# Two background streams with buffers of their own for the weight gradients and the x gradient in a fused decode-block backward kernel

## The chip, the cores and the metric

The kernel runs on one core of a Trainium2 chip. The metric is the device time of one execution in microseconds. The core has five engines with a queue each, worked through in order: TensorE (PE) multiplies matrices and writes PSUM, VectorE (DVE) and ScalarE (ACT) work elementwise and read PSUM, GpSimd (POOL) and SyncE (SP) mostly issue DMA transfers here. Sixteen DMA engines move data between HBM and the on-chip SBUF.

## What is computed

The reference is a transformer block for one new token per sequence, and its gradients. There are B = 2 sequences, D = 640, 32 heads of 128, a cache of 4096 positions, and a hidden width of 1728.

```
h   = x + attention(layernorm(x) @ wq, k_cache, v_cache) @ wo
out = h + relu(layernorm(h) @ w1) @ w2
grads of out, by grad_out, for x, k_cache, v_cache, wq, wo, w1, w2
```

Outputs are out_0 (out), out_1 (gradient of x), out_2 and out_3 (of the two caches, 64 blocks of 1 MB each), out_4 (wq), out_5 (wo), out_6 (w1) and out_7 (w2), all bf16. The weight gradients are sums of two outer products, one for each sequence.

## The kernel before

**Passes.** A head of a sequence is a pair, and there are 64. The first pass (p1_iter) loads K and V of a pair, makes scores, softmax and the attention output. Two sequences' worth of middle work (middle_gen: output projection, layer norm, the hidden layer and its gradient, and from that the gradient at each head's output, go_group) runs as a background generator. The second pass (p2_iter, L740) loads V of a pair once more as tile W, except for 11 pairs whose V was kept. It transposes W in four groups on PE (t_ps, copied by ACT to t_sb), multiplies each with the head's gradient (dp_ps), and DVE forms the blocks gV and gK as outer products in two halves each (L735). POOL issues their stores (L792, L773). The pass has an iteration j for each pair; the store of gK for pair j stands in iteration j+1. Iterations j = 0 to 10 are interleaved with the first pass, j = 11 to 64 stand alone.

**Background work.** All order is set while the program is written out. p2_iter is a generator with yields between its parts; after each part the loop writes out V loads as far as buffers allow (pump, L998) and then steps of background queues. A queue has a credit that grows by a rate per step; a background generator yields the price of what it wrote out (a plain yield is 0.5), and is called until the credit is used up (bg_step, L945). The counter step[0] counts steps of the second queue, and wait(n) lets n of them pass (2n in the lone second pass). What bg2 holds is fin_gen (L847), at the rate RATE2 = 0.85, from the iteration in which the middle work of the second sequence no longer needs w1.

**What fin_gen does.** rows_of (L799) turns column vectors into rows: ACT widens four columns (L805), PE transposes them (L810), ACT copies them out (L812). outer_rows (L818) makes a weight gradient in groups of rows: a buffer ot of 1 MB or less is taken, PE forms pieces of up to 512 columns (L835), three of them in three PSUM banks, ACT copies the three into ot (L840), and POOL issues the store (L842). The order is out_7, out_6, out_5, the rest of gx, out_1, out_4. Between stores of out_6 and out_5, gx_piece (L856) runs once the heads it needs are done: it loads six heads of wq (tile wqs, L862, from SP), waits 12 steps, transposes 128x128 blocks on PE (L873), ACT copies them (L875), PE multiplies with the query gradient (L885), and DVE adds (L889).

**Buffers.** SBUF has 12 large buffers of 1 MB. They have homes: "ld" for loads (K, V, W, wq, w2 and also ot and wqs) and "g" for gV and gK. take and give move them; a buffer that is given back can be taken at once, and then its next writer waits on the chip until its last reader, or its store, is done. share(4) and share(5) move homes from "ld" to "g" at the start of the lone second pass and at j = 37. `spare` is the number of free "ld" buffers that background work must find (2, from j = 34 on 1), and `reserve` keeps 2 from the V loads from j = 36 on. w1 lies in a pool of its own, wts; when it is released, the pool fin (rows and small tiles) takes its place.

Of the kernel before, what the change touches and what calls it, by code (L numbers as in the profile page):

```python
# [15 lines left out]
def kernel(  # L16
# [60 lines left out]
    homes = {"ld": list(range(NBIG)), "g": []}  # L77
    free = {"ld": NBIG, "g": 0}
    owned = {"ld": NBIG, "g": 0}
    stores = [0]  # L80
    spare = [2]
    home_of = {}

    def take(tag, shape, name):
        assert free[tag] > 0, (tag, name)
        free[tag] -= 1
        k = homes[tag].pop(0)
        t = big.tile(shape, BF16, tag=f"big{k}", bufs=1, name=name)
        home_of[id(t)] = (tag, k, t)
        return t  # L90

    def give(t, to=None):
        tag, k, _ = home_of.pop(id(t))
        to = to or tag
        owned[tag] -= 1
        owned[to] += 1
        free[to] += 1
        homes[to].append(k)

    def share(n):  # L100

        stores[0] = n
        while owned["g"] < n and free["ld"] > 0:
            homes["g"].append(homes["ld"].pop(0))
            for d in (free, owned):
                d["ld"] -= 1
                d["g"] += 1
# [464 lines left out]
    def store_row(col_bf, n, dst):  # L572

        t = pst([16, 128], BF16, "mid", "row_ps")
        nc.tensor.transpose(t[0:n, :], col_bf, ident_bf[:])
        r = small.tile([16, 128], BF16, tag="orow", bufs=1, name="orow")
        nc.vector.tensor_copy(out=r[0:n, :], in_=t[0:n, :])
        nc.sync.dma_start(out=dst, in_=r[0:n, :])
# [47 lines left out]
    def mlp_out():  # L626

        ml32 = small.tile([128, ND, B], FP32, tag="ml32", bufs=1, name="ml32")
        nc.vector.memset(ml32[:], 0.0)
        for k in range(NW2):  # L630
            while free["ld"] < spare[0]:
                yield
            t = load_w2(k, "ld")
            yield from wait(8)
            c1 = min(NF, (k + 1) * FP)
            m_ps = pst([128, ND, B], FP32, "mid", "mlp_ps")
            for c in range(ND):
                for cf in range(k * FP, c1):
                    kc = f_kc(cf)
                    nc.tensor.matmul(m_ps[:, c, :], lhsT=t[0:kc, cf - k * FP, c * 128:(c + 1) * 128],  # L640
                                     rhs=acol[0:kc, cf, :], start=(cf == k * FP), stop=(cf == c1 - 1))
            give(t)
            yield
            nc.vector.tensor_tensor(out=ml32[:], in0=m_ps[:], in1=ml32[:], op=ALU.add)
        ml_bf = small.tile([128, ND, B], BF16, tag="ml_bf", bufs=1, name="ml_bf")
        nc.vector.tensor_copy(out=ml_bf[:], in_=ml32[:])
        y_bf = small.tile([128, B, ND], BF16, tag="y_bf", bufs=1, name="y_bf")
        nc.vector.tensor_tensor(out=y_bf[:].rearrange("p b c -> p c b"), in0=h1c[:], in1=ml_bf[:], op=ALU.add)
        yield from wait(3)
        for b in range(B):  # L650
            store_row(y_bf[:, b, :], ND, out_0[b].rearrange("s (c p) -> (s c) p", p=128))
            yield
# [87 lines left out]
    def p2_iter(j, busy):  # L740
# [45 lines left out]
        give(c["W"], "g" if owned["g"] < stores[0] else "ld")  # L786
# [31 lines left out]
    def outer_rows(L, nrow, R, N, out_ap, cc, between=None):  # L818


        P = nrow // cc
        grp = max(1, min(cc, 4096 // N))
        out_v = out_ap.rearrange("(p c) n -> p c n", c=cc)
        for c0 in range(0, cc, grp):
            gn = min(grp, cc - c0)
            while free["ld"] < spare[0]:
                yield
            ot = take("ld", [128, grp, N], "ot")
            todo = [(k, n0, min(512, N - n0)) for k in range(gn) for n0 in range(0, N, 512)]
            for t0 in range(0, len(todo), 3):  # L830
                part = []
                for k, n0, nn in todo[t0:t0 + 3]:
                    q = 32 * (fw[0] % 4)
                    o_ps = pst([128, 512], FP32, ("mid", "m", "a")[len(part)], "o_ps")
                    nc.tensor.matmul(o_ps[0:P, 0:nn], lhsT=L[q:q + B, bass.ds(c0 + k, P, step=cc)],  # L835
                                     rhs=R[q:q + B, n0:n0 + nn], start=True, stop=True)
                    part.append((o_ps, k, n0, nn))
                    fw[0] += 1
                for o_ps, k, n0, nn in part:
                    nc.scalar.copy(out=ot[0:P, k, n0:n0 + nn], in_=o_ps[0:P, 0:nn])  # L840
                yield 0.5 * len(part)
            nc.gpsimd.dma_start(out=out_v[:, c0:c0 + gn, :], in_=ot[0:P, 0:gn, :])  # L842
            give(ot)
            if between is not None:
                yield from between()

    def fin_gen(fin):  # L847
        gx1 = fin.tile([128, ND, B], FP32, tag="gx1", name="gx1")
        nc.vector.memset(gx1[:], 0.0)
# [3 lines left out]
        yield from wait(4)  # L853
        gx_next = [0]

        def gx_piece(k):  # L856

            hn = min(QP, H - k * QP)
            while free["ld"] < spare[0]:
                yield  # L860
            t = take("ld", [128, ND, QP * 128], "wqs")
            nc.sync.dma_start(out=t[:, :, 0:hn * 128], in_=wq_r[:, :, k * QP * 128:(k * QP + hn) * 128])  # L862
            yield from wait(6)
# [3 lines left out]
            for t0 in range(0, len(todo) + GT, GT):  # L867
                part = todo[t0:t0 + GT]
                nxt = None
                if part:  # L870
                    t_ps = pst([128, GT, 128], BF16, "tps", "t_ps")
                    for x, (c, j) in enumerate(part):
                        nc.tensor.transpose(t_ps[:, x, :], t[:, c, j * 128:(j + 1) * 128], ident_bf[:])  # L873
                    t_sb = mats.tile([128, GT, 128], BF16, tag="XT", bufs=5, name="t_sb")
                    nc.scalar.copy(out=t_sb[:, 0:len(part), :], in_=t_ps[:, 0:len(part), :])  # L875
                    nxt = (t_sb, part)
                    if t0 + GT >= len(todo):
                        give(t)
                    yield 0.9
                if prev is not None:  # L880
                    if acc is None:
                        acc = pst([128, ND, B], FP32, "m", "gx_ps")
# [4 lines left out]
                    yield  # L887
                prev = nxt
            nc.vector.tensor_tensor(out=gx1[:], in0=gx1[:], in1=acc[:], op=ALU.add)  # L889

        def gx_ready():

            k = gx_next[0]
            if k < NQ and all(("go", B - 1, h) in done for h in range(k * QP, min(H, (k + 1) * QP))):
                gx_next[0] += 1
                yield from gx_piece(k)

        yield from rows_of(fin, acol, NF, "ar", "rF")
        yield from rows_of(fin, gc, ND, "gr", "rD")
        yield from outer_rows(FIN["ar"], Dff, FIN["gr"], D, out_7, Dff // 96)  # L900
        yield from rows_of(fin, ghfc, NF, "ghfr", "rF")
        yield from rows_of(fin, x2c, ND, "x2r", "rD")
        yield from outer_rows(FIN["x2r"], D, FIN["ghfr"], Dff, out_6, ND, gx_ready)
        while ("gh1", B - 1) not in done:
            yield
        yield from rows_of(fin, OFc, H, "OFr", "rH")
        yield from rows_of(fin, gh1c, ND, "gh1r", "rD")
        yield from outer_rows(FIN["OFr"], HD, FIN["gh1r"], D, out_5, HD // 128, gx_ready)
        while gx_next[0] < NQ:
            yield from gx_ready()  # L910
# [5 lines left out]
        for b in range(B):  # L916
            gxo = small.tile([128, ND], BF16, tag="gxo", bufs=2, name="gxo")
            nc.vector.tensor_copy(out=gxo[:], in_=gx_bf[:, :, b])
            store_row(gxo[:], ND, out_1[b].rearrange("s (c p) -> (s c) p", p=128))
            yield  # L920
        yield from rows_of(fin, GQc, H, "GQr", "rH")
        yield from rows_of(fin, x1c, ND, "x1r", "rD")
        yield from outer_rows(FIN["x1r"], D, FIN["GQr"], HD, out_4, ND)
# [3 lines left out]
    bg2 = []  # L927
    done = set()
    credit = [0.0, 0.0]
# [15 lines left out]
    def bg_step(k, rate):  # L945
        step[0] += k
        q = (bg, bg2)[k]
# [17 lines left out]
    RATE2 = 0.85  # L965
# [30 lines left out]
    reserve = [0]  # L996

    def pump():  # L998
        while queue:
# [3 lines left out]
            else:  # L1003
                tag = "ld"
                if free["ld"] <= reserve[0]:
# [12 lines left out]
    fin = None  # L1018
# [12 lines left out]
    for n, (i, j) in enumerate(plan):  # L1031
# [3 lines left out]
        if j == 0:  # L1035
            stores[0] = 3
        if i is None and plan[n - 1][0] is not None:
            share(4)
        if j == H + KEPT[1]:
            share(5)  # L1040
# [6 lines left out]
        reserve[0] = 2 if bg2 and j is not None and j >= H + 4 else 0  # L1047
        spare[0] = 1 if j is not None and j >= H + 2 else 2
        if i is None and ("w1", 1) in done and fin is None:
            wts.release()  # L1050
            fin = tc.alloc_tile_pool(name="fin", bufs=1)
            bg2.append(("fin", fin_gen(fin)))
        if i == 12:
# [3 lines left out]
        if i is None:  # L1057
            spread[0] = 2
            k = 0
            while g2 is not None:  # L1060
# [5 lines left out]
                bg_step(1, RATE2)  # L1066
            continue
        at = MIXED if j is not None else REST
        for k, _ in enumerate(p1_iter(i, i < H + 1, int(H + 1 < i < P2_AT))):
# [15 lines left out]
            bg_step(1, RATE2)  # L1085
# [4 lines left out]
    while bg2:  # L1090
        bg_one(bg2)
# [32 lines left out]
```

## Time and profile before

| | |
|---|---|
| median of 13 runs | 1008.92 us (1003.01 to 1024.74) |
| time of the profiled execution | 1012.83 us |
| its span, first to last instruction | 1011.0 us |
| busy: PE, DVE, ACT, POOL | 799.5, 657.3, 586.8, 108.6 us |
| granted TensorE clock, mean | 0.783 |
| moved by DMA | 363.25 MB, 359 GB/s over the span |
| last gV store issued, last gK store issued | 951.43, 959.23 us |
| last weight-gradient store issued | 1004.55 us |
| first weight-gradient copy (out_7) | 701.4 us |
| wqs loads: issue to landing, min/median/max | 17.7/24.6/31.5 us |
| ot stores: issue to landing, min/median/max | 4.1/6.2/19.5 us |

Two views are read together. One gives, for a stretch of the span, each engine's busy time with the number of its instructions, the granted clock, the mean busy share of the DMA engines and the rate at which they moved data. The other, the timeline, gives each instruction's start and length, and in brackets how long its engine was idle before it and what ended that. A line of the waits names an engine and line, what it waited for, the total, the number of times and the longest. Line numbers are those of the code above.

### The profile page before, as it was taken

The page shows a single profiled execution, that of the slowest core. Times are in us where ns is not written, and L with a number is a line of the kernel's source. Part 1 is how long each engine was busy: PE and PEld are TensorE (multiplying, and loading weights), DVE is VectorE, ACT ScalarE, POOL GpSimd, SP SyncE. Part 2 cuts the span into 40 slices and gives each one's busy share as a digit, 9 for nine tenths or more (in the row PEclk, how much of TensorE's full clock was granted, in tenths as well). Part 3 has the DMA queues.
Part 4 walks back from the last instruction along what each step waited for, and adds up shares of the span by engine and source line. Part 5 has one row for each costly group of instructions (what it writes and reads, how often), then busy time and mean ns, then how long its engine had stood idle before and what let it go on. Part 6 is the DMA issues. An engine that isn't in the chain of part 4 may idle for free.

```text
span 1011.0 us, 30245 instructions
## 1 busy us (share of the span) xinstructions
PE 799.5 (79%) x13169; PEld 707.8 (70%) x13173; DVE 657.3 (65%) x1289; ACT 586.8 (58%) x1261; POOL 108.6 (11%) x219
## 2 busy tenths in 40 slices
PE   6999989999899989999886736467487578865846
PEld 5998989988888888888876636356366467654611
DVE  3555766755387668787888798998675456653600
ACT  4566655666667757777754524345365347644747
POOL 0000000000000000000012121112122112210201
PEclk9999997999699979999995856776556557555555
DMA  9999999994677779999999999999799998999735
GB/s 350 419 398 381 361 377 376 364 389 169 218 262 269 287 287 369 422 420 421 405 381 421 424 379 405 426 423 420 307 375 410 420 414 328 421 424 414 300 128 207
DMA packets 63206, 363.25 MB, mean 359 GB/s; under 512 B 5697, under 2 KB 20929, under 8 KB 22881
## 3 DMA queue, kind: packets, MB, share of 16 engines
q1 hardware_dynamic: 42416, 212.18, 54.0%
q0 software_dynamic: 20656, 149.14, 35.6%
q8 instruction: 103, 1.69, 0.6%
q14 instruction: 31, 0.25, 0.1%
HBM read 212.16 MB, written 149.13 MB: 357 GB/s over the span
## 4 chain that ended last, share of the span: by engine, by line
PE 44%; DMA 28%; issue 10%; DVE 10%; ACT 7%; POOL 1%; SPq 0%; POOLq 0%; DVEq 0%; ACTq 0%
PE t_ps L353 11%; PE m_ps L408 11%; DMA wqs<-in_A_wq_dram 10%; DMA out_dram<-gV 8%; DMA out_dram<-gK 7%; PE t_ps L374 5%; PE m_ps L423 5%; ACT t_sb L358 4%; PE s_ps L364 4%; DVE gV L735 4%; DVE gK L735 3%; DMA Kt<-in_A_k_cache_dram 2%; PE dp_ps L387 1%; PE t_ps L345 1%; PE t_ps L873 1%
## 5 line engine op out<-in xcount | busy, mean ns | idle before, releaser
L358 ACT COPY t_sb<-t_ps 128x1024 bf16<-128x1024 bf16 x223 | 219.6, 1014 | 52.7 <-PE t_ps L353 50.4
L379 ACT COPY t_sb<-t_ps 128x512 f32<-128x512 f32 x256 | 148.7, 588 | 114.2 <-PE t_ps L374 111.2
L408 PE MATMUL m_ps<-pk,Vt 128*128 128x129 bf16 x2048 | 204.3, 228 | 4.0 <-issue 4.0
L374 PE MATMUL t_ps<-ident_f,Wt 128*128 128x128 f32 x848 | 186.4, 368 | 2.0 <-DMA Wt<-in_A_v_cache_dram 1.0
L415 DVE TENSOR_TENSOR pk<-Kt,ep 128x2048 bf16<-128x2048 bf16 x128 | 156.0, 1219 | 26.5 <-ACT ep L465 26.5
L735 DVE TENSOR_TENSOR gK<-rb,gsp 128x2048 bf16<-128x2048 bf16 x128 | 152.1, 1227 | 32.1 <-DMA out_dram<-gV 16.9
L735 DVE TENSOR_TENSOR gV<-rb,pp 128x2048 bf16<-128x2048 bf16 x128 | 152.2, 1217 | 22.7 <-DMA out_dram<-gK 11.8
L353 PE MATMUL t_ps<-ident_bf,Kt 128*128 128x128 bf16 x2048 | 158.6, 230 | 4.0 <-issue 2.0
L408 PEld LDWEIGHTS <-Vt 128*128 128x128 bf16 x2048 | 135.6, 103 | 14.3 <-issue 9.0
L374 PEld LDWEIGHTS t_ps<-ident_f,Wt 128*128 128x128 f32 x848 | 132.5, 190 | 16.8 <-issue 8.6
L353 PEld LDWEIGHTS <-Kt 128*128 128x128 bf16 x2048 | 132.3, 103 | 7.2 <-issue 2.9
L387 PEld LDWEIGHTS <-t_sb 128*128 128x128 bf16 x2048 | 92.0, 105 | 50.3 <-ACT t_sb L379 39.7
L387 PE MATMUL dp_ps<-gom,t_sb 128*128 128x2 bf16 x2048 | 94.5, 167 | 23.0 <-ACT t_sb L379 21.9
L364 PE MATMUL s_ps<-qc,t_sb 128*128 128x1 bf16 x2048 | 89.7, 164 | 12.6 <-ACT t_sb L358 8.6
L364 PEld LDWEIGHTS <-t_sb 128*128 128x128 bf16 x2048 | 80.9, 98 | 17.8 <-ACT t_sb L358 12.8
L840 ACT CAST ot<-o_ps 128x512 bf16<-128x512 f32 (+4 forms) x160 | 66.0, 491 | 22.9 <-DMA out_dram<-ot 13.5
L792 POOL DMA_DIRECT2D out_dram<-gV x64 | 34.2, 534 | 386.3 <-DVE gV L735 289.8
L356 DVE COPY t_sb<-t_ps 128x1024 bf16<-128x1024 bf16 x33 | 22.8, 691 | 67.9 <-PE t_ps L353 67.9
L518 ACT ACTIVATE MT<-m_ps,rtot 128x128 bf16<-128x128 f32 x64 | 23.6, 368 | 71.6 <-PE m_ps L408 67.3
L423 PE MATMUL m_ps<-ep,Kt 128*128 128x1 bf16 x2048 | 61.2, 163 | 1.8 <-ACT OU L519 1.2
L773 POOL DMA_DIRECT2D out_dram<-gK x64 | 34.0, 532 | 262.9 <-DVE gK L735 216.9
L423 PEld LDWEIGHTS <-Kt 128*128 128x128 bf16 x2048 | 58.9, 96 | 2.2 <-issue 1.7
(186 smaller groups left out, 878.8 us busy)
## 6 DMA issues: line engine op xcount, KB each, us to landing
Kt<-in_A_k_cache_dram SPq DMA_DIRECT2D x64, 1024.0 KB, 9.7
Vt<-in_A_v_cache_dram SPq DMA_DIRECT2D x64, 1024.0 KB, 8.3
out_dram<-gV POOLq DMA_DIRECT2D x64, 1024.0 KB, 10.9
out_dram<-gK POOLq DMA_DIRECT2D x64, 1024.0 KB, 10.2
Wt<-in_A_v_cache_dram SPq DMA_DIRECT2D x53, 1024.0 KB, 10.7
wo_t<-in_A_wo_dram SPq DMA_DIRECT2D x4, 1280.0 KB, 11.2
out_dram<-ot POOLq DMA_DIRECT2D x5, 1024.0 KB, 4.1
wq_t<-in_A_wq_dram SPq DMA_DIRECT2D x5, 960.0 KB, 9.5
```

Of the source, the lines that this page charges most:

```text
L353: nc.tensor.transpose(t_ps[:, j, :], nat[:, g * GT + j, :], ident_bf[:])
L358: nc.scalar.copy(out=t_sb[:], in_=t_ps[:])
L364: nc.tensor.matmul(dst[:, sc:sc + 1], lhsT=t_sb[:, j, :], rhs=vec, start=True, stop=True)
L374: nc.tensor.transpose(t_ps[:, j, :], natf[:, 2 * cc:2 * cc + 2, :].rearrange("p c k -> p (c k)"), ident_f[:])
L379: nc.scalar.copy(out=t_sb[:], in_=t_ps[:])
L387: nc.tensor.matmul(dst[:, sc:sc + 2], lhsT=v[:, j, :, par], rhs=vecs[:, par, :], start=(par == 0), stop=(par == 1))
L408: nc.tensor.matmul(r["m"][:, 0:129], lhsT=r["V"][:, sc, :], rhs=r["pk"][sc // HALF][:, sc % HALF, 0:129], start=False, stop=(sc == NSC - 1))
L415: nc.vector.tensor_tensor(out=p["pk"][k][:, :, 0:128].rearrange("p s (a two) -> p s a two", two=2), in0=p["K"][:, sl, :].rearrange("p s (a ...
L423: nc.tensor.matmul(r["m"][:, 129:130], lhsT=r["K"][:, sc, :], rhs=r["ep"][:, sc, 0:1], start=(sc == 0), stop=False)
L735: nc.vector.tensor_tensor(out=pairs_view(dst[:, sl, :]), in0=row.rearrange("p (a two) -> p a two", two=2)[:, None, :, :].to_broadcast([128 ...
L792: nc.gpsimd.dma_start(out=natural(out_3, b, h), in_=gV[:])
L840: nc.scalar.copy(out=ot[0:P, k, n0:n0 + nn], in_=o_ps[0:P, 0:nn])
```

## The change

The homes become four: "ld", "g", "f" for weight-gradient buffers (ot) and "q" for wqs and for the w2 tiles of mlp_out. share takes a wanted number for each home, and free or returned buffers move towards it. One more large buffer is added in the pool big2, in w1's old place (fin shrinks, since rows of 4096 columns are made in halves). It is the only "f" buffer until j = 36, when the kept V tiles are used up and the numbers become ld 4, g 4, f 3, q 2; when both streams have ended they become ld 7, g 6. A buffer of "f" is taken only 13 steps after it was given back.

fin_gen loses gx, which becomes gx_gen on a third queue, bg3, with the rate 0.45; RATE2 is 0.65. gx_gen starts when all heads are done and takes a "q" buffer and loads the next piece of wq whenever one is free. outer_rows makes one piece at a time in the bank "m"; gx's sums use the bank "a". From when all heads are done (late), DVE makes every third copy. Stores of ot are issued by ACT instead of POOL. out_5 and out_4 are made in two halves of 16 heads, and out_4 no longer stands behind the end of gx. orow gets two buffers.

```diff
     NBIG = 12
-    homes = {"ld": list(range(NBIG)), "g": []}
+    homes = {"ld": list(range(NBIG)), "g": [], "f": [], "q": []}
...
+    def goes_to(tag):
+
+        if owned[tag] > wanted.get(tag, NBIG):
+            for other in homes:
+                if owned[other] < wanted.get(other, 0):
+                    return other
+        return tag
+
     def give(t, to=None):
         tag, k, _ = home_of.pop(id(t))
-        to = to or tag
+        to = to or goes_to(tag)
...
+        given_at[k] = step[0]
+
+    def rested(tag, n):
+
+        return free[tag] > 0 and (forced[0] or step[0] >= given_at.get(homes[tag][0], -n) + n)
...
         for k in range(NW2):
-            while free["ld"] < spare[0]:
+            while free["q"] < 1:
                 yield
-            t = load_w2(k, "ld")
+            t = load_w2(k, "q")
...
-    def outer_rows(L, nrow, R, N, out_ap, cc, between=None):
+    def outer_rows(L, nrow, R, N, out_ap, cc):
...
-            while free["ld"] < spare[0]:
-                yield
-            ot = take("ld", [128, grp, N], "ot")
+            while not rested("f", 13):
+                yield 0.0
+            ot = take("f", [128, grp, N], "ot")
...
+            for x, (k, n0, nn) in enumerate(todo):
+                q = 32 * (fw[0] % 4)
+                fw[0] += 1
+                o_ps = pst([128, 512], FP32, "m", "o_ps")
+                nc.tensor.matmul(o_ps[0:P, 0:nn], lhsT=L[q:q + B, bass.ds(c0 + k, P, step=cc)],
+                                 rhs=R[q:q + B, n0:n0 + nn], start=True, stop=True)
+                yield 0.3
+                if late[0] and x % 3 == 0 and x < len(todo) - 1:
+                    nc.vector.tensor_copy(out=ot[0:P, k, n0:n0 + nn], in_=o_ps[0:P, 0:nn])
+                else:
                     nc.scalar.copy(out=ot[0:P, k, n0:n0 + nn], in_=o_ps[0:P, 0:nn])
-                yield 0.5 * len(part)
-            nc.gpsimd.dma_start(out=out_v[:, c0:c0 + gn, :], in_=ot[0:P, 0:gn, :])
+                yield 0.3
+            nc.scalar.dma_start(out=out_v[:, c0:c0 + gn, :], in_=ot[0:P, 0:gn, :])
             give(ot)
...
+    def gx_gen(fin):
...
+        def fetch():
+            while len(tiles) < NQ and free["q"] > 0:
+                k = len(tiles)
+                hn = min(QP, H - k * QP)
+                t = take("q", [128, ND, QP * 128], "wqs")
+                nc.sync.dma_start(out=t[:, :, 0:hn * 128], in_=wq_r[:, :, k * QP * 128:(k * QP + hn) * 128])
+                tiles.append(t)
+
+        while not all(("go", B - 1, h) in done for h in range(H)):
+            yield 0.0
+        while not tiles:
+            fetch()
+            yield
+        yield from wait(7)
+        for k in range(NQ):
+            while k >= len(tiles):
+                fetch()
+                yield
+            t = tiles[k]
...
                     if t0 + GT >= len(todo):
                         give(t)
+                        fetch()
                     yield 0.9
...
-    RATE2 = 0.85
+    RATE2 = 0.65
+    RATE3 = 0.45
...
         if i is None and plan[n - 1][0] is not None:
-            share(4)
-        if j == H + KEPT[1]:
-            share(5)
+            share(ld=KEPT[1] + 3, g=4)
+        if fin is not None and not bg2 and not bg3:
+            share(ld=7, g=6)
+        elif fin is not None and j >= H + KEPT[1] - 1:
+            share(ld=4, g=4, f=3, q=2)
...
             fin = tc.alloc_tile_pool(name="fin", bufs=1)
+            big2 = tc.alloc_tile_pool(name="big2", bufs=1)
+            more_home("f", big2)
             bg2.append(("fin", fin_gen(fin)))
+            bg3.append(("gx", gx_gen(fin)))
+        late[0] = all(("go", B - 1, h) in done for h in range(H))
```

## The prediction

> **What bounds the kernel now.** I first read the page's rows in 40 slices, then cut the span into stretches and asked each for engine time and DMA rate, then the waits and the timeline of the stretches where the rate falls.
>
> ```profile
> PEclk9999997999699979999995856776556557555555
> DMA  9999999994677779999999999999799998999735
> ```
>
> From the twentieth slice on the sixteen DMA engines are almost always full while the granted TensorE clock lies near a half. The table by stretch (columns: stretch, length, busy time of PE, PEld, DVE, ACT and POOL, granted clock, DMA share, GB/s) says how full:
>
> ```profile
> 594.00:612.00 18.00, 13.94 (x144) 12.64 (x144) 17.69 (x32) 10.12 (x26) 4.10 (x7) 0.54 0.91 335
> 612.00:708.00 96.00, 59.54 (x716) 50.55 (x715) 82.29 (x140) 39.54 (x79) 18.12 (x38) 0.69 1.01 423
> 708.00:750.00 42.00, 25.00 (x239) 19.84 (x236) 30.93 (x51) 21.13 (x53) 8.73 (x18) 0.54 0.86 327
> 750.00:834.00 84.00, 57.90 (x654) 49.03 (x654) 43.53 (x59) 39.51 (x74) 16.56 (x29) 0.56 1.02 414
> 834.00:846.00 12.00, 11.18 (x132) 10.20 (x133) 8.31 (x11) 7.65 (x14) 2.29 (x4) 0.50 0.64 217
> 846.00:924.00 78.00, 51.99 (x579) 42.41 (x578) 43.69 (x45) 41.88 (x91) 14.60 (x31) 0.61 1.01 424
> 924.00:960.00 36.00, 32.20 (x299) 23.68 (x297) 22.97 (x29) 25.69 (x58) 6.27 (x14) 0.55 0.82 332
> 960.00:1011.00 51.00, 26.58 (x87) 8.20 (x85) 1.70 (x10) 29.28 (x68) 4.02 (x8) 0.50 0.41 169
> ```
>
> The reader is to see a ceiling, 423 GB/s for 96 us on end, and five stretches below it. Against 423, a stretch of length T at rate r has lost T x (1 - r/423): 3.7 us in 594-612, 9.5 in 708-750, 1.8 in 750-834, 5.8 in 834-846, 7.7 in 924-960 and 30.6 in 960-1011: 59.1 us. With the same bytes and every stretch full, the span would be 1011.0 - 59.1 = 951.9 us. The waits name the reasons. Times are start, length, with the idle time in brackets:
>
> ```profile
> 723.34 2.18 ACT L840 CAST ot<-o_ps 96x512 bf16<-96x512 f32 x6 [13.54 <-DMA out_dram<-ot]
> 806.50 1.89 PE L873 MATMUL t_ps<-ident_bf,wqs 128*128 128x128 bf16 x16 [10.89 <-DMA wqs<-in_A_wq_dram]
> 987.78 0.53 POOL L842 DMA_DIRECT2D out_dram<-ot  x1 [24.43 <-ACT ot L840]
> SPq L395 <- DMA out_dram<-ot: 112.7, 5, 38.4
> ```
>
> A weight-gradient buffer reused at once held ACT for 13.54 us, and PE and the DMA with it (the 708-750 dip). The loads of wq come just before use, so PE waits. In the end the five stores of out_4 stand alone, made at ACT's pace of one per 4.2 us, with 24 us of rows and layer norm ahead of them in which almost nothing is stored. Loads of V wait in SP's queue for 112.7 us until ot buffers come free.
>
> **The change part by part.** Up to iteration j=20 of the second pass (about 594 us, where the fin work starts) nothing differs in order.
>
> *Earlier weight gradients.* out_7 began at 701 us though its rows were ready at 611 us: it waited for a spare load buffer. It now has a buffer in w1's place. By the code an iteration of the second pass has 7 steps. At 0.65 credit a step, 160 pieces of 0.6 and 32 row chunks of 1.7 are 150.4 credits, 231 steps, 33 iterations; adding the rests of 13 steps while there is one buffer (four waits, before j=38), I count the end at j=59.4. The gx stream starts in j=40-41 (the last go group: GQc at 756.7, between the products of j=39 and j=40), takes 5.6 credits a piece at 0.45, 12.4 steps, and ends at j=56; the three w2 pieces end at j=58.6. The second pass runs to j=64: nothing is left behind it. So the 30.6 us go, and 7.7 us with them, but for an end: 6.4 us from the issue of the last 1 MB store (1004.55) to the end of the span, less 2.5 for its own bytes, and about 3 for the last four iterations, whose 2.1 MB (5.0 us) come at PE's pace of 5.6 to 6.0 us (rb copies at 935.22, 940.78 and 946.76). End: 7 us.
>
> *Buffers that rest.* Thirteen steps are 1.9 iterations, 15 us at 8 us an iteration and 19 at 10.2; ot stores landed in 4.1 to 19.5 us, 6.2 in the middle. I take the 13.54 us wait as gone with its 9.5 us of DMA. SP no longer has a V load behind an ot store (the 112.7 us).
>
> *wq loaded two pieces ahead.* By the count each piece is loaded 2 to 3.4 iterations, 20 to 34 us, ahead; such loads took 17.7 to 31.5 us, 24.6 in the middle. A few us of PE waiting stay, under a full DMA. The 5.8 us of 834-846 go. Behind PE's wait everything of the second pass is queued, so if loads are later than that, the dip returns: 5.8 us each, at most six.
>
> *V loads with four buffers, g with four instead of five.* Four loads of 1 MB ahead are some 40 us; median landing is 10.7. Cost nothing while the DMA is full; bounds 0 to 5 us, I take 0.
>
> *Stores on ACT's queue.* 18 issues. No row has one on ACT; on SP an issue takes 0.37 us, on POOL 0.53: 7 to 10 us of ACT, which is half idle. Nothing on the path; the last piece's copy is ACT's own. What waits behind it is a t_sb copy, so PE would see 0.5 us each, 9 us in all if never hidden, covered by the full DMA.
>
> *One PSUM bank for the pieces.* This costs. Before, three matmuls filled three banks and three copies followed. Now matmul and copy alternate on one bank, 2.17 of them a step; going through the credit by hand (3, 2, 2, 2, 2, 2), in 7 of 12 steps a copy stands right ahead of the next matmul, and PE, in order, waits for it. From the timeline at 938: transposes end, 0.09, t_sb copy 0.59, ot copy 0.59 less 0.4 of matvecs: 0.9 us in the four steps with transposes, about 0.65 in the others, 0.8 on average. 7 x 7/12 x 0.8 = 3.3 us an iteration. While out_5 and gx run together (8.2 iterations): second pass 4.9 (its PE work from 940.14 to 945.01), gx 3.0 (per piece 30 transposes and matvecs, 5.3 us, in 1.78 iterations), 7.6 pieces at 0.21 make 1.6, the waits 3.3: 12.8 us of PE at half clock. The DMA needs 2.10 + 1.05 + 0.62 + 0.55 = 4.32 MB, 10.2 us. For out_4 (5.1 iterations): 4.9 + 7.6 x 0.43 + 3.3 = 11.5 against 4.14 MB, 9.8 us. Lost: 8.2 x 2.6 + 5.1 x 1.7 = 30 us at half clock. At full clock (four transposes 0.66 instead of 1.09) PE needs 10.0 and 8.7 and loses 0. The stretch with the densest such work, 846-858, was granted 1.00, the whole of 846-924 0.61; I take 0.7: 18 us, with 0 and 30 as ends.
>
> *A third of the copies on DVE once go is done.* No row has a DVE copy of this shape; L356 copies 1024 bf16 from PSUM in 0.69 us. Some 36 pieces at 0.3 to 0.7 us: DVE has room (44 of 78 us busy). One can sit behind a 1.22 us half product, at most 36 x 1.22 = 44 us of PE waiting, at least nothing; ACT is spared as much. PE has 0.4 to 1.1 us an iteration to spare where its clock is up, so I take 0; the far end belongs to the third rival.
>
> *Not touched:* 3.7 us in 594-612, where DVE is busy 17.69 of 18 us, and 1.8 us of mixed packets.
>
> **Sum.** 951.9 + 3.7 + 1.8 + 7 + 18 = 982.4 us of span, 28.6 less. The profiled run took 1012.83 us (1.83 around the span); it was 0.39% above the median of the runs, 1008.92. (1012.83 - 28.6) x 1008.92 / 1012.83 = **980 us**.
>
> The Trainium skill ("DMA: Bandwidth & Descriptors", "Where 436 GB/s comes from") names about 358 GB/s as a core's share of HBM, and says that this side binds for transfers between HBM and SBUF; by that, 363 MB need 1015 us and the change can bring nothing. The row of 612-708 stands at 423, so here the trace decides. The same page ("Queues, rings and completion order") says that a DMA engine takes turns between the queues that have work; by that a third queue would leave gK and gV a third of 423, 141 GB/s, where an iteration of 10.2 us wants 206. No view of before has three busy queues; buffers that rest should keep the new one short of work.
>
> **Rivals.**
> - *PE chained at half clock all through.* For: clocks of 0.50 to 0.61 in most stretches after 708. Against: 1.00 in 846-858. It gives the 30 us, and 8 more where a gx copy of 1.01 us stands before the piece's copy: span 1002.4, time 1000. Chance 0.16.
> - *ACT blocked by its own stores.* If an ot store lands after more than 13 steps, the 13.54 us wait returns; each cost the DMA 5.6 us (720-732: 12 us at 226 GB/s). For: 19.5 us was seen. Against: the middle is 6.2. Five of the 15 reuses would eat the gain of 28.6 us: 1009. Chance 0.06.
> - *Slower: the single bank stops PE at every piece.* A wait of 1.0 us in all seven steps, and DVE pieces behind half products (2.7 us an iteration): 16.5 us against 10.2 for out_5, 17.9 against 9.8 for out_4, 93 us lost, span 1057, time about 1055. It decides from 46.6 us, 3.5 an iteration over 13.3, and what I expect is 1.4. For: pieces of P2 wait in the same PE queue. Against: the credits put matmul and copy in the same order only half the time. Chance 0.13, partly near 1020.
> - *Better.* No wait of PE shows, and the end is shorter: 955 to 962. Chance 0.06.
>
> **How the numbers follow.** The forecast, 962 to 992 by the ends 0 and 30 of its last term, has 0.59. With the first rival and half of the better case the range is 959 to 1004. A measurement of this kernel tells 0.3% from no change, 1006 to 1012. Faster: 0.59 + 0.16 + 0.06 and a little of the second, 0.82; same 0.04; slower 0.14.
>
> **What would show it.** Right: no span without stores after the last gK; out_4 stored before j=63; rates above 400 GB/s in most stretches from 700 on; ACT's wait for an ot landing gone; PE waits for ot copies of a few us an iteration. Wrong: ot stores behind the last gK (the count of steps), PE waits for wqs over 10 us with low DMA (the loads), or rates near 330 where out_5 and gx run together (the bank), which beyond 46 us would turn the sign.

## The result, and the profile after

The changed kernel took 1029.34 us in the median of 11 runs (1026.26 to 1038.98), against 1009.14 us for the kernel before over all its runs: a ratio of 1.0214, with a 95% interval of 1.0186 to 1.0241. It is 2.1% slower, where 980 us had been forecast. Runs more than 1.5% above the fastest of their kernel are left out of all ratios and of the medians of the experiments; the profiled runs of two experiments, all copies on ACT in the changed kernel and no rest, are such runs. The profiled execution of the changed kernel took 1035.96 us, with a span of 1034.1 us.

The table by stretch of the changed kernel has the columns of the one shown for before:

```profile
594.00:612.00 18.00, 10.07 (x109) 8.65 (x110) 15.59 (x29) 8.36 (x22) 4.10 (x8) 0.62 0.98 380
612.00:708.00 96.00, 72.24 (x627) 56.46 (x625) 73.30 (x127) 48.12 (x106) 16.15 (x33) 0.53 0.99 382
708.00:750.00 42.00, 33.19 (x283) 24.80 (x282) 31.24 (x48) 22.39 (x45) 7.08 (x14) 0.54 0.91 371
750.00:834.00 84.00, 60.46 (x596) 46.62 (x594) 44.86 (x69) 40.20 (x84) 11.17 (x23) 0.53 0.89 340
834.00:924.00 90.00, 60.82 (x645) 45.22 (x642) 41.67 (x63) 43.44 (x86) 9.14 (x21) 0.62 0.78 283
924.00:1011.00 87.00, 64.50 (x488) 42.86 (x484) 52.00 (x66) 39.22 (x76) 12.38 (x25) 0.53 0.95 363
1011.00:1034.00 23.00, 6.85 (x108) 5.63 (x108) 12.63 (x14) 5.34 (x11) 4.17 (x8) 0.71 0.84 350
```

The empty end is gone: nothing lies at 169 GB/s any more, the last weight-gradient store is issued at 1000.98 us and the last gK store at 1025.62. But no stretch reaches 423 GB/s either. Counted as in the prediction, T x (1 - r/423), the stretches from 594 on lose 1.8, 9.3, 5.2, 16.5, 29.8, 12.3 and 4.0 us, 79 in all, more than the 59 of before. The loss is no longer at a few places; it is spread over the whole lone second pass, and largest in 834-924, where out_5 and the x gradient run beside it. The waits of PE in that time (who waited, for what, us, times, longest) name the new reasons:

```profile
PE o_ps L859 <- ACT ot L865: 61.5, 85, 1.7
PE t_ps L929 <- DMA wqs<-in_A_wq_dram: 17.6, 3, 7.1
PE o_ps L859 <- DVE ot L863: 13.5, 18, 2.0
```

For 103 of the 160 pieces PE stands still until the piece before has been copied out of the one PSUM bank: 75.0 us, 0.73 us each. In the kernel before, three banks left 19.1 us of such waits, and 14.0 of them are a single wait, behind the ACT copy that a store held up:

```profile
PE o_ps L835 <- ACT ot L840: 19.1, 12, 14.0
```

How one of them comes about is seen in the timeline of PE and then of ACT in the changed kernel, while out_7 is made:

```profile
618.95 1.11 PE L397 MATMUL t_ps<-ident_f,Wt 128*128 128x128 f32 x4
619.85 0.40 PE L410 MATMUL dp_ps<-gom,t_sb 128*128 128x2 bf16 x8
620.95 0.58 PE L859 MATMUL o_ps<-gr,ar 2*96 2x512 bf16 x1 [0.70 <-ACT ot L865]
621.46 1.11 PE L397 MATMUL t_ps<-ident_f,Wt 128*128 128x128 f32 x4
```

```profile
620.15 0.59 ACT L402 COPY t_sb<-t_ps 128x512 f32<-128x512 f32 x1 [1.44 <-PE t_ps L397]
620.63 0.26 ACT L865 CAST ot<-o_ps 96x128 bf16<-96x128 f32 x1
622.66 0.59 ACT L402 COPY t_sb<-t_ps 128x512 f32<-128x512 f32 x1 [1.77 <-PE t_ps L397]
```

The copy of the piece before (620.63) stands on ACT behind the t_sb copy, which waits for PE's transposes; PE, which has nothing else in front of the next piece, waits for both. From one group of transposes to the next 2.51 us pass (618.95 to 621.46), where a group with no piece between took 1.15 us before (937.16 to 938.31):

```profile
937.16 1.09 PE L374 MATMUL t_ps<-ident_f,Wt 128*128 128x128 f32 x4
938.05 0.40 PE L387 MATMUL dp_ps<-gom,t_sb 128*128 128x2 bf16 x8
938.31 1.09 PE L374 MATMUL t_ps<-ident_f,Wt 128*128 128x128 f32 x4
```

### The profile page after: what moved, and what is told of

Read it like the earlier page. It is cut to its first block, busy times and chain, and to the rows that moved or that the text cites. A ratio compares the mean times of both kernels' runs of the same rounds, so it can differ in the third digit from the quotient of the medians.

```text
span 1034.1 us, 30153 instructions
## 1 busy us (share of the span) xinstructions
PE 832.4 (80%) x13169; PEld 723.5 (70%) x13173; DVE 675.7 (65%) x1322; ACT 579.5 (56%) x1228; POOL 97.4 (9%) x202
## 4 chain that ended last, share of the span: by engine, by line
PE 56%; DMA 15%; ACT 14%; DVE 8%; issue 5%; POOL 0%; SPq 0%; ACTq 0%; POOLq 0%; DVEq 0%
PE t_ps L397 11%; PE t_ps L376 10%; PE m_ps L431 10%; DMA out_dram<-gV 6%; PE o_ps L859 6%; PE m_ps L446 4%; ACT t_sb L381 4%; PE s_ps L387 4%; ACT ot L865 3%; DMA wqs<-in_A_wq_dram 3%; DVE gV L758 3%; DMA out_dram<-gK 2%; ACT t_sb L402 2%; PE dp_ps L410 2%; DMA Kt<-in_A_k_cache_dram 2%
## 5 line engine op out<-in xcount | busy, mean ns | idle before, releaser
L397 PE MATMUL t_ps<-ident_f,Wt 128*128 128x128 f32 x848 | 196.6, 381 | 1.7 <-DMA Wt<-in_A_v_cache_dram 1.4
L397 PEld LDWEIGHTS t_ps<-ident_f,Wt 128*128 128x128 f32 x848 | 138.2, 197 | 55.1 <-issue 40.4
L376 PE MATMUL t_ps<-ident_bf,Kt 128*128 128x128 bf16 x2048 | 155.8, 227 | 5.4 <-issue 3.3
L376 PEld LDWEIGHTS <-Kt 128*128 128x128 bf16 x2048 | 129.3, 102 | 9.2 <-issue 4.8
L410 PEld LDWEIGHTS <-t_sb 128*128 128x128 bf16 x2048 | 97.0, 107 | 49.5 <-ACT t_sb L402 24.9
L387 PEld LDWEIGHTS <-t_sb 128*128 128x128 bf16 x2048 | 80.3, 98 | 19.7 <-ACT t_sb L381 13.6
L865 ACT CAST ot<-o_ps 128x512 bf16<-128x512 f32 (+2 forms) x127 | 60.1, 473 | 44.5 <-PE o_ps L859 43.4
L771 DVE SCALAR_TENSOR_TENSOR gsp<-dp_ps,negdot,P_bf 128x64 bf16<-128x64 f32 x64 | 18.0, 281 | 68.2 <-PE dp_ps L410 67.9
```

Source lines behind the costliest of these rows:

```text
L376: nc.tensor.transpose(t_ps[:, j, :], nat[:, g * GT + j, :], ident_bf[:])
L387: nc.tensor.matmul(dst[:, sc:sc + 1], lhsT=t_sb[:, j, :], rhs=vec, start=True, stop=True)
L397: nc.tensor.transpose(t_ps[:, j, :], natf[:, 2 * cc:2 * cc + 2, :].rearrange("p c k -> p (c k)"), ident_f[:])
L410: nc.tensor.matmul(dst[:, sc:sc + 2], lhsT=v[:, j, :, par], rhs=vecs[:, par, :], start=(par == 0), stop=(par == 1))
```

## The experiments

All times are medians; the kernel before took 1008.2 to 1010.9 us beside them. The theory after the result was the single bank: matmul, copy and next matmul form a chain across two engines that work in order, and the second pass, written into the same two queues, waits with them. Its rivals were the stores on ACT's queue, the DVE copies, and the loads of wq.

**Copy right behind its matmul.** The order on the one bank, and nothing else:

```diff
                                  rhs=R[q:q + B, n0:n0 + nn], start=True, stop=True)
-                yield 0.3
...
-                yield 0.3
+                yield 0.6
```

> The changed kernel with one edit: each piece's copy is written right behind its matmul, and then 0.6 credits are paid, so that a copy seldom stands right ahead of the next matmul. Banks, buffers, queues and work stay. Theory (PE waits for the copy out of the single bank): the 75 us that PE waits at L859 for ot copies fall to under 25, and the time falls by 30 to 60 us, to 970 to 1000. Rival (the stores on ACT's queue or the third DMA queue slow the stores): 1029, within 5. Rival (the loads of wq come late since w2 holds one of the two buffers): 1029, within 5.

Measured: 1008.74 us, ratio 0.9966 (0.992 to 1.0011) to before. The waits fell to 47.8 us, so 27 us less of waiting gave 21 us of time, and neither rival can have had those 21. Both are less than expected.

```profile
PE o_ps L859 <- ACT ot L864: 38.5, 56, 3.9
PE o_ps L859 <- DVE ot L862: 9.3, 15, 0.8
```

The timeline of PE in this kernel shows one place where waits are left: several pieces follow each other with nothing of the second pass between. By the code, credit that has gathered in a pause puts them into one step.

```profile
628.81 0.26 PE L859 MATMUL o_ps<-gr,ar 2*96 2x128 bf16 x1 [0.67 <-ACT ot L864]
629.41 0.58 PE L859 MATMUL o_ps<-gr,ar 2*96 2x512 bf16 x1 [0.35 <-ACT ot L864]
630.66 0.26 PE L859 MATMUL o_ps<-gr,ar 2*96 2x128 bf16 x1 [0.67 <-ACT ot L864]
```

**Copy always right ahead of the next matmul**, the opposite dose (0.6 credits between matmul and copy, none after):

> The changed kernel with the copy of a piece always written right ahead of the next piece's matmul (0.6 credits lie between matmul and copy, none between copy and next matmul). Nothing else differs. Theory (single bank): PE now waits at nearly all of the 160 pieces instead of 103, so its waits for ot copies grow from 75 to some 110 to 130 us and the time by 20 to 45 us, to 1050 to 1075. Rival (what the pair order won came from elsewhere, such as earlier copies or a shorter stream): 1029, within 8.

Measured: 1054.56 us, ratio 1.0446 (1.0341 to 1.0551). PE's waits rose to 110.3 us at 135 pieces:

```profile
PE o_ps L859 <- ACT ot L865: 92.3, 114, 3.9
PE o_ps L859 <- DVE ot L863: 18.0, 21, 2.0
```

With the same bank, buffers, queues and work, the place of one yield moves the time from 1009 over 1029 to 1055, while the waits go from 48 over 75 to 110 us: some 0.7 us of time for a us of waiting. PE's waits for wqs go the other way (21.2, 17.6 and 9.6 us), so they are not the reason.

**The single bank alone, in the kernel before:**

```diff
-                    o_ps = pst([128, 512], FP32, ("mid", "m", "a")[len(part)], "o_ps")
+                o_ps = pst([128, 512], FP32, "m", "o_ps")
...
+                yield 0.25
                 nc.scalar.copy(out=ot[0:P, k, n0:n0 + nn], in_=o_ps[0:P, 0:nn])
+                yield 0.25
```

> The kernel before with one part of the change alone: its pieces go one at a time through the bank m, matmul, 0.25 credits, copy, 0.25 credits, instead of three at a time through three banks. Theory (single bank): at the end, where the 40 pieces of out_4 stand alone, a piece takes about 1.25 us instead of 0.52, 25 to 35 us more; while the second pass runs, 120 pieces cost PE up to 0.7 us each, part of it under full DMA: 10 to 50 us more. Together 1045 to 1090. Rival (the single bank is harmless, the loss of the change is in its buffers, queues and streams): under 1020.

Measured: 1068.09 us, ratio 1.0583 (1.0492 to 1.0675). PE waited 90.0 us for ACT's copies. At the end, where out_4 stands alone, a piece takes 1.25 us, as the timeline of this kernel has it (1041.46 to 1042.71), against 0.52 in three banks:

```profile
1041.46 0.58 PE L834 MATMUL o_ps<-GQr,x1r 2*128 2x512 bf16 x1 [0.67 <-ACT ot L837]
1042.71 0.58 PE L834 MATMUL o_ps<-GQr,x1r 2*128 2x512 bf16 x1 [0.67 <-ACT ot L837]
```

That is 29 us for the 40 pieces, of 54.7 us between the spans of the two profiled runs (1065.7 and 1011.0). Another 19 us came while the second pass ran: the last gK store is issued at 978.0 us instead of 959.2. The remaining 7 us lie between the two.

**Two banks.** Pieces go by turns through m and mid, with the copy right behind. Two reads of mid stand a step earlier for it:

```diff
-                o_ps = pst([128, 512], FP32, "m", "o_ps")
+                o_ps = pst([128, 512], FP32, ("m", "mid")[fw[0] % 2], "o_ps")
...
         t = colsum(mm[:].rearrange("p a b -> p (a b)"), 2 * nb)
-        yield
...
                                 scalar1=-1.0 / D, scalar2=None, op0=ALU.mult)
+        yield
...
             give(t)
-            yield
             nc.vector.tensor_tensor(out=ml32[:], in0=m_ps[:], in1=ml32[:], op=ALU.add)
+            yield
```

> The changed kernel with the pieces going alternately through two banks, m and mid, copy right behind matmul, 0.6 credits a piece; so that mid is free, two small reads of mid (layer norm's sums, the output's sum) stand one step earlier. Theory (single bank): the 48 us of waits that the pair order alone left, which stand where several pieces follow each other in a step, fall under 15, and the time from 1009 to 985 to 1000. Rival (after the pair order the bank is no longer the limit): 1009, within 5.

Measured: 996.89 us, ratio 0.9863 (0.9767 to 0.9958): 32 us below the changed kernel and in the range expected. PE's waits for copies of pieces are 15.1 us (13.0 and 2.1). The interval overlaps that of the pair order on one bank, so how the 32 us divide between order and bank is not settled. And another wait has grown to be the first:

```profile
PE t_ps L928 <- DMA wqs<-in_A_wq_dram: 33.9, 5, 8.4
PE o_ps L859 <- ACT ot L864: 13.0, 16, 3.3
```

**wq first.** SP's timeline in the changed kernel shows why wqs comes late. Its first load is written right behind a load of w2 for the output, and each further one only after the piece before it is finished:

```profile
775.78 0.43 SPq L323 DMA_DIRECT2D w_t<-in_B_w_dram  x1
776.26 0.54 SPq L905 DMA_DIRECT2D wqs<-in_A_wq_dram  x1
...
805.97 0.38 SPq L323 DMA_DIRECT2D w_t<-in_B_w_dram  x1
812.66 0.38 SPq L905 DMA_DIRECT2D wqs<-in_A_wq_dram  x1
...
833.27 0.33 SPq L323 DMA_DIRECT2D w_t<-in_B_w_dram  x1
833.65 0.48 SPq L326 DMA_DIRECT2D w_t<-in_B_w_dram  x1
834.24 0.53 SPq L905 DMA_DIRECT2D wqs<-in_A_wq_dram  x1
```

The w2 tile and gx had one "q" buffer each, so gx, which was meant to have two, had nothing to load ahead with. The edit holds mlp_out back until all six pieces are loaded:

```diff
-            while free["q"] < 1:
+            while free["q"] < 1 or not gx_loaded[0]:
...
                 tiles.append(t)
+                gx_loaded[0] = len(tiles) == NQ
```

> The changed kernel with the w2 pieces of the output held back until all six pieces of wq have been loaded, so that gx has both of its buffers from the start. PE's 17.6 us of waiting for wqs fall to under 8. Theory (single bank): 5 to 15 us less, 1014 to 1024. Rival (late loads of wq are the main loss): back to 1009 or below.

Measured, on the changed kernel: 1018.49 us, ratio 1.0122 (1.0078 to 1.0165), 11 us less; PE has no wait for wqs left, while its waits for copies of pieces stay at 72.9 us. And with both edits together:

> The kernel with two banks and copies right behind matmuls, and the w2 pieces held back until all of wq is loaded. If the two causes add up (the bank, and the late loads of wq, which alone were worth 9 us): 975 to 992, faster than the kernel before. If they hide each other: as with two banks alone, within 4. If PE's own work beside the second pass is now the limit: 995 to 1005 in spite of few waits.

Measured: 978.36 us, ratio 0.9672 (0.9596 to 0.9747). The two add up (32 and 11 against 51); the 8 us more lie within the intervals. The table of this kernel, and its waits:

```profile
594.00:700.00 106.00, 78.74 (x732) 62.05 (x732) 85.18 (x143) 55.72 (x127) 18.17 (x39) 0.56 0.98 386
700.00:780.00 80.00, 67.83 (x610) 52.62 (x609) 61.69 (x98) 47.01 (x100) 17.25 (x30) 0.54 0.98 390
780.00:920.00 140.00, 114.01 (x1164) 86.08 (x1162) 84.32 (x115) 81.44 (x161) 20.61 (x41) 0.59 1.01 407
920.00:975.00 55.00, 31.21 (x333) 23.68 (x332) 35.98 (x43) 20.97 (x39) 9.76 (x20) 0.62 0.95 394
```

```profile
PE t_ps L930 <- DMA wqs<-in_A_wq_dram: 17.6, 2, 9.1
PE o_ps L860 <- ACT ot L865: 13.0, 16, 2.2
```

In 780-920 the DMA carries 407 GB/s, where the changed kernel has 314 and the kernel before 403; and nothing is left behind the second pass.

**The loads of wq earlier still:** the first two pieces of wq are loaded as soon as "q" buffers are free.

```diff
         while not all(("go", B - 1, h) in done for h in range(H)):
+            fetch()
             yield 0.0
```

> The kernel with two banks and wq first (978), with the first two pieces of wq loaded as soon as their buffers are free, not only when all heads are done. PE's 17.6 us of waiting for wqs stand at later pieces too, so 0 to 6 us less: 972 to 978.

Measured: 977.24 us, ratio 0.9699 (0.9654 to 0.9744). PE's waits for wqs fell from 17.6 to 8.6 us, and the time did not move beyond its interval. These two kernels are the fastest here, 3% below before.

**No rest.** The kernel with two banks and wq first, with `rested("f", 0)` for `rested("f", 13)`:

> The kernel with two banks and wq first (978), with no rest: a weight-gradient buffer may be taken in the step in which it was given back. If the rests of 13 steps are what keeps ACT from waiting for its own stores, ACT waits some 5 to 14 us at the four reuses of the single buffer before j = 38, and the time is 985 to 1010. If stores land soon enough anyway (2.4 to 10.3 us in the changed kernel): 978, within 5.

Measured: 1000.59 us, ratio 0.9926 (0.989 to 0.9961), 22 us more than with rests. In the profiled execution (1018.7 us) ACT waits for its own stores at 640, 666, 714 and 732 us, the four reuses of the single buffer that the prediction had counted:

```profile
ACT ot L865 <- DMA out_dram<-ot: 38.4, 4, 10.6
```

With rests this wait is 2.3 us at two places. Over these four waits, from the 25th to the 33rd gK store, this execution falls 35 us further behind the one with rests. By the medians 13 steps are worth some 22 us here; whether fewer would do was not tried.

**The stores' queue.** ot stores by POOL instead of ACT, on the changed kernel and then on the fast one:

```diff
-            nc.scalar.dma_start(out=out_v[:, c0:c0 + gn, :], in_=ot[0:P, 0:gn, :])
+            nc.gpsimd.dma_start(out=out_v[:, c0:c0 + gn, :], in_=ot[0:P, 0:gn, :])
```

> The changed kernel with the ot stores issued by POOL, as before. Theory (single bank): 1029, within 5. Rival (ACT's queue, or a third DMA queue that takes turns with the others): 1000 to 1012, most of the loss undone.

> The kernel with two banks and wq first (978), with the weight-gradient stores issued by POOL. With the bank out of the way the queue of the stores may show: if ACT's queue helps, POOL's stores of gK and gV wait behind a store that waits for ACT, 982 to 995; if it doesn't matter, as in the changed kernel, 978, within 5.

Measured: 1030.17 us (ratio 1.0183, 1.0094 to 1.0272) against 1029, and 978.34 (0.9708, 0.9666 to 0.9749) against 978. The queue makes no difference to the time that can be seen, in either kernel. It does to the waits: with POOL's stores in the fast kernel ACT waits 16.8 us for its own stores, at three places, and PE 26.8 us for ACT's copies, without a loss of time. So a us of such waiting doesn't always cost time.

**The copies on DVE.** All copies of pieces on ACT, again on both:

```diff
-                if late[0] and x % 3 == 0 and x < len(todo) - 1:
+                if False and late[0] and x % 3 == 0 and x < len(todo) - 1:
```

> The changed kernel with every copy of a piece on ACT, none on DVE. Theory (single bank): the waits for DVE's copies (13.5 us of PE, 55 us of DVE ahead of gK and gV) are replaced by waits for ACT's; a gain of 5 to 15 us, to 1014 to 1024, since the chain over the one bank stays. Rival (DVE copies alone are the loss): back to 1009 or below.

> The kernel with two banks and wq first (978), with every copy of a piece on ACT, none on DVE. With two banks a copy that sits behind a half product on DVE holds no matmul up: a gain or a loss under 6 us, 972 to 984. If DVE's 34 us of waiting for pieces ahead of gK and gV counts: 960 to 972.

Measured: 1027.54 us (ratio 1.0158, 1.0044 to 1.0273), and 979.99 (0.974, 0.968 to 0.98). No gain is seen, where 5 to 15 us were expected in the first; its interval is too wide to exclude them. PE's waits for copies are 77.1 us, all of them for ACT, instead of 75.0 for both. The waits change their owner, as the bank stays one.

## Why the prediction was wrong, point by point

- **The ceiling and the empty end: right.** The end after the last gK is gone in every version of the changed kernel. With the two faults mended the DMA reaches 422 to 423 GB/s again in three stretches of 30 us (774-804, 834-864, 924-954). That this kernel's 978 us lie beside the forecast 980 is luck: the forecast holds 18 us for the single bank, which this kernel doesn't have. Without them the sum gives 962 us, and 16 us stay open.
- **"Nothing is left behind it", the count of steps: right.** The last ot store (1000.98) lies before the last gK (1025.62), between the gK stores of iterations 59 and 60, where j=59.4 had been counted.
- **"Buffers that rest": right.** ACT waits 0.2 us for its own stores in the changed kernel. The rests save the fast version 22 us, more than the step's 9.5, since the new stream has four such reuses and not one.
- **"V loads with four buffers" at nothing: right.** In the second pass PE waits for a V load once, 1.4 us (1.0 before).
- **"Stores on ACT's queue" and "a third of the copies on DVE" at nothing: right** within the intervals of the two pairs of runs.
- **"One PSUM bank for the pieces ... 18 us, with 0 and 30 as ends": this step failed, by its size.** The wait of a piece was well put (0.8 us forecast, 0.73 measured; 7 waits in 12 steps, which make 13 pieces, forecast, 103 of 160 pieces measured). What the waits cost was not: two banks and the pair order give 32 us back (1029.3 to 996.9), and 40 us where the loads of wq are in time (1018.5 to 978.4). Two choices made the term small. The clock was taken as 0.7; the stretches show 0.53, 0.54, 0.53, 0.62 and 0.53, nearly the half clock whose price was 30 us. And the waits were priced for out_5 and out_4 alone. The step said of no wait in out_7 and out_6, and a full DMA was to cover them; those two have 26.6 of the 75 us (17.8 and 8.8), and 612-708 went from 423 to 382 GB/s.
- **Where that loss lies.** The gK stores of the two kernels with wq first place it: from the 23rd to the 41st (out_7 and out_6) 154.2 us with one bank and 145.7 with two, from there to the last (out_5, gx, out_4) 247.4 and 212.9. That is 8 us where nothing was priced, and 34 where the price at half clock was 30.
- **The low clock by itself is not the loss.** By the step's own sum PE needs 12.8 - 3.3 = 9.5 us an iteration without the waits, under the DMA's 10.2, and the fast version takes 978 us at clocks of 0.54 to 0.62.
- **"Each piece is loaded 2 to 3.4 iterations ahead": this step failed, in its mechanism.** PE was to wait "a few us"; it waits 17.6 us (40.3 before). The count gave gx both "q" buffers at the start. mlp_out, in the queue that is stepped first, took one of them for w2, and each load of wq came when it was needed. The step's warning, "if loads are later than that, the dip returns", had the right sign; priced there at 5.8 us each, at most six, it would have been up to 35 us. It is worth 11 us in the changed kernel and 19 with two banks (996.9 to 978.4).
- **The signs of being wrong.** Two of those named came: PE waits for wqs over 10 us, and 283 GB/s, below the 330 named, where out_5 and gx run together.
- **The rivals.** The third had the sign and the mechanism (the bank stops PE) and asked for a wait of 1.0 us at every step; 0.73 at 64% of the pieces sufficed for the sign. Its sum for out_5 leaves out the 2.7 us of the DVE pieces that its sum for out_4 has; with them it would have been about 115 us lost and not 93. It decides from 46.6 us, and the two faults together cost 51 (1029.3 to 978.4). With only the late loads the kernel takes 996.9 us, with only the bank 1018.5: the bank by itself decides the sign. The first rival's condition, a clock near a half, came too, without its time of 1000 us; the second, ACT blocked by its own stores, didn't come.

What stays open: how the gain of the two banks divides between bank and order, and what holds the fast version's first 186 us after 594 at 386 to 390 GB/s, where before had 408 and 368 in the same two stretches. The 16 us above the sum may lie there; no run shows it.

## What to carry to other kernels

When background work is woven into the instruction queues of a tight loop, count for each piece what stands directly ahead of it on the engine it needs: a chain of matmul, copy, matmul through one PSUM bank makes the loop wait for the copy wherever the copy stands directly ahead of the next matmul. Here a better place of one yield took 27 of 75 us of such waits away, and a second bank with it 60. Price such waits over the whole stretch where they occur, also where a full DMA seems to cover them, and at the clock that the profile of that stretch shows. When two streams share buffers, write down which one asks first.

## What the hardware showed that was not expected

- The granted clock didn't follow PE's busy share. In the fast version (two banks, wq first) PE is busy 114 of 140 us in 780-920 at a clock of 0.59; the kernel before had 9.6 of 12 us in 846-858 at 1.00. No run here shows what sets it.
- In the changed kernel a 512-column copy out of PSUM takes 0.69 us on DVE and 0.59 on ACT; an issue of a store on ACT 0.35 us, 18 of them in all.
- The round trip of a piece through one bank, in the kernel before with the single bank alone, is hardly longer than its parts: 1.25 us, of which the matmul's 0.58 and the copy's 0.59 are all but 0.08.
